# Sums of v for eight blocks a visit, and six dense matmuls in a row behind each visit

## The chip, the cores and the metric

The kernel runs on one core of a Trainium2 chip. The time is the device time of one execution in microseconds; the median of 3 runs of the kernel before is 846.09 us (845.69 to 846.45). The core has engines with a queue each that work side by side: TensorE (PE, with its weight loads shown apart as PEld), VectorE (DVE), ScalarE (ACT), GpSimd (POOL), and SyncE (SP), which issues most of the DMAs. PE writes its results to PSUM, from where DVE and ACT read them.

## The reference

Two mixers run on the same x (2048 positions, width 512) and are blended by a gate for each position. A is a Fourier transform along both axes of which the real part is kept; B is attention with 32 heads of 16 and a causal window of 256 positions. Cut to what matters:

```python
def A(x, dft_seq_re, dft_seq_im, dft_hid_re, dft_hid_im):
    a = jnp.einsum("bsd,ed->bse", x, dft_hid_re)
    b = jnp.einsum("bsd,ed->bse", x, dft_hid_im)
    return jnp.einsum("ts,bse->bte", dft_seq_re, a) - jnp.einsum("ts,bse->bte", dft_seq_im, b)

def B(x, wqkv, wo):
    # H = 32, Dh = 16, W = 256, S = 2048, D = 512
    q, k, v = split_heads(x @ wqkv)
    scores = einsum("bhqd,bhkd->bhqk", q, k) * Dh ** -0.5
    scores = where((i - j >= 0) & (i - j < W), scores, -1e9)
    o = einsum("bhqk,bhkd->bhqd", softmax(scores), v)
    return merge_heads(o) @ wo

x = A_x
g = sigmoid((x * gate_w).sum(-1, keepdims=True))
out = g * A(x, ...) + (1 - g) * B(x, B_wqkv, B_wo)
```

## The kernel before, in words

**Dense work.** Products of float32 accuracy are made of three float32r matmuls: an operand is split into `hi` (a rounded copy) and `lo` (the rest), and hi*hi, hi*lo and lo*hi are added in PSUM. The generator `dense` yields after each such matmul of 512 columns: the projections of q and k (`dqk`), of v (`dv`), of x by the hidden DFT matrices (`dab`), and then the sequence DFT (`dc`), which takes most of the kernel. The sequence matrices come in 64 pieces of 128x1024; a piece is loaded (`Pieces.load`, tile `raw`, two buffers), split into a `hi` and a `lo` tile of pool `st` (three buffers of each), and used by 24 matmuls (8 chunks of 3). The split of the next piece is put in four jobs (hi and lo of each half) that `job` hands to DVE at the matmuls 3, 9, 15 and 21 of the piece before it; in the tail the hi copies go to ACT. The first half of a piece is used by its matmuls 1 to 12, the second by 13 to 24; lo is first read by the third matmul of a half.

**Attention.** There are four groups of 8 heads and 32 blocks of 64 queries in each, 128 blocks in all, n = 0 to 127. Every block has four parts p. `s_pair(n, p)` makes scores (`s`), whose row minimum DVE finds (`sm`, line 369) and whose exponentials ACT sums (line 372): it gives the softmax's maximum and sum. 19 blocks later (`LAG`), as block k = n - 19, `t_pair(k, p)` makes the transposed scores with the maximum already in (`t`), of which ACT writes the exponentials to a tile `PT[k]` (line 450), and POOL clears what lies outside the window (lines 454, 458). `s`, `t` and a small turn of the statistics share four PSUM buffers (`ps_a`) in turn: a tile takes the buffer of the fourth before it.

**Sums of v.** `pv(k)` multiplies `PT[k]` with v in plain float32, each matmul 32 columns of the array wide (`o`, line 475), into one of two PSUM tiles of 512 queries; `v` stands for four blocks at a time in one of two tiles `vpad`, spread by POOL. `pv` is not called block by block: the main loop calls it for all blocks that have gathered, in a *visit*, at the start of block n: four blocks at first, six once the projections have ended and the tile `home` has room for some `PT`, two at the end. `PT` lies in four buffers of pool `at` and then also in two places of `home`. When eight blocks are summed, `o_out` multiplies the PSUM tile by the inverse sums (DVE, line 496) and stores it.

**Order on PE.** PE's order is the order of the program. The loop goes over n and p: `s_pair`, a gap, `t_pair`, a gap, and in each gap `fill` takes dense matmuls from the generator, two for n in 19 to 127, one or two for other n. At a visit (p = 0) both gaps come ahead of it, and `t_pair(k, 0)` stands behind it, directly ahead of the next `s_pair`. The other engines' orders are made by a scheduler, from the program's order and the helpers `behind` and `late`.

**After the attention** (`attention_done`) what is left of the sequence DFT runs with the output projection between its chunks (`tail_step`, matmuls `t` of line 922); free tiles (`vpad`, pads) take the attention's results (`oraw`).

Of the kernel before, what the change touches and what calls it, by code (L numbers as in the profile page):

```python
# [14 lines left out]
P = 128  # L15
# [17 lines left out]
def fnet_window_mix(ctx: ExitStack, tc: tile.TileContext, xT, x, wqk, wv, wr, wi, cr, ci, wo, gw, out):  # L33
    nc = tc.nc

    const = ctx.enter_context(tc.tile_pool(name="const", bufs=1))
    big = ctx.enter_context(tc.tile_pool(name="big", bufs=16))
    st = ctx.enter_context(tc.tile_pool(name="st", bufs=3))
    ev = ctx.enter_context(tc.tile_pool(name="ev", bufs=5))
# [18 lines left out]
    def f(ap):  # L58
        return ap.bitcast(F32)
# [33 lines left out]

    HALVES = slice(0, 512), slice(512, 1024)

    def load_raw(src):
# [4 lines left out]
    def split_raw(raw, act=False):  # L101
        hi = st.tile([P, 1024], F32R, name="hi")
        lo = st.tile([P, 1024], F32R, name="lo")
        for c in HALVES:
            split(hi[:, c], lo[:, c], raw[:, c], act)
        return hi, lo
# [4 lines left out]
    def split_soon(raw):  # L111
        hi = st.tile([P, 1024], F32R, name="hi")
        lo = st.tile([P, 1024], F32R, name="lo")
        for c in HALVES:
# [4 lines left out]

    def job(n):  # L120
        if n == 2 and ended:
            ended.pop(0)()
        if n % 6 == 3 and jobs:
            jobs.pop(0)()
# [22 lines left out]
    with tc.manual_schedule(engines={mybir.EngineType.Activation, mybir.EngineType.DVE, mybir.EngineType.SP}):  # L147
        wraw, *xraw = [pt_raw() for _ in range(3)]
        wq0 = [st.tile([P, 1024], F32R, name=h) for h in ("hi", "lo")]
        zero = ev.tile([P, 512], F32R, name="ev")  # L150
# [71 lines left out]
    g1 = const.tile([P, 16], F32, name="g1")  # L222
    g0 = const.tile([P, 16], F32, name="g0")
    gwb = []

# [11 lines left out]
    def gate(tb):  # L237
# [3 lines left out]
        if tb == 15:  # L241
            e = const.tile([P, 16], F32, name="ge")
# [7 lines left out]

    home = const.tile([P, 3072], F32R, name="home")
    turn = iter(range(99))
# [159 lines left out]
    PT = {}  # L412
    more = []

    VR = {}
# [108 lines left out]
    def c_part(w, chunks, ab, ps, ends):  # L524
        for i in chunks:
            if FIN and i % 2 == 0:
                tail_step()
            for n, (a, b) in enumerate(TERMS):
                nc.tensor.matmul(ps, w[a][:, i % 8 * 128:i % 8 * 128 + 128], ab[SC[i]][:, b],  # L529
                                 start=i == ends[0] and a + b == 0, stop=i == ends[1] and a == 1)  # L530
                job(i % 8 * 3 + n + 1)
                if i != chunks[-1] or a == 0:
# [50 lines left out]

    have = set()

# [9 lines left out]
    def dense():  # L595
# [83 lines left out]
        for sb in range(16):  # L679
# [280 lines left out]
    stream = dense()  # L960
    quota = 0.0

    def need(key):
# [57 lines left out]
    for n in range(N + LAG + 1):  # L1021
# [10 lines left out]
        for p in range(NP):  # L1032
            if n < N:
                s_pair(n, p)
            fill(n)
            visit = p == 0 and (k - summed >= (6 if more else 4) or k == N)
            if 0 <= k < N and not visit:
# [6 lines left out]
            if visit:  # L1044
# [68 lines left out]
```

## Time and profile before

| What | Value |
|---|---|
| median of 3 runs | 846.09 us (845.69 to 846.45) |
| the profiled execution | 845.1 us, its span 843.3 us |
| PE busy | 838.5 us, 99% |
| PEld busy | 695.8 us, 83% |
| DVE busy | 643.8 us, 76% |
| ACT busy | 611.1 us, 72% |
| POOL busy | 298.8 us, 35% |
| granted TensorE clock | 1.000 |
| DMA | 161.03 MB, mean 191 GB/s |

The span runs from the first to the last instruction. A matmul's recorded time overlaps with the next one's, since they are pipelined, so what a matmul costs is read from the distance of two starts and not from its duration. A row of the timeline has the start in us, the duration in us, the engine, the line, the operation, what it writes and reads, the shape, a count, and in brackets how long its engine sat idle before it and what ended that. Rows that follow each other with the same line and tiles are merged, with the count behind the x. Between the start of a merged row of matmuls and the next row lies what all of them took.

### The profile page before, as it was taken

Reading aid. Unit: us, or ns where it says so; the run is one execution under the profiler, and the core shown is the slowest. Engines: PE = TensorE matmul, PEld = TensorE weight load, DVE = VectorE, ACT = ScalarE, POOL = GpSimd, SP = SyncE. Lnnn points to the kernel's source line nnn. Section 1 sums busy time; section 2 is a strip of 40 time slices with the busy share of each in tenths; the row PEclk is TensorE's granted clock in tenths of the full one; section 3 lists DMA queues with packets and bytes.
Section 4 is the critical chain, followed back from the end, with each engine's and each line's share of the span. In section 5 each row is a group of like instructions: output and inputs, shape, how many; then the busy total and the mean of one; then the engine's idle time right before and its main releaser. Section 6 shows DMA issues by size and latency. Waiting matters only on the chain.

```text
span 843.3 us, 17171 instructions
## 1 busy us (share of the span) xinstructions
PE 838.5 (99%) x5310; PEld 695.8 (83%) x5310; DVE 643.8 (76%) x2083; ACT 611.1 (72%) x1832; POOL 298.8 (35%) x606
## 2 busy tenths in 40 slices
PE   9999999999999999999999999999999999999998
PEld 7888888888888888888888887878887878878997
DVE  5588978677979787787877877878987867666874
ACT  6488888878888897787877977867777865553430
POOL 8102333233232233342333243343242357756410
PEclk9999999999999999999999999999999999999999
DMA  8776678485766173534454547979874256455732
GB/s 295 251 227 187 217 243 283 159 259 202 220 222 189 54 232 107 177 120 121 140 160 126 168 153 223 298 214 309 274 216 149 96 179 198 137 192 196 220 133 92
DMA packets 94475, 161.03 MB, mean 191 GB/s; under 512 B 26800, under 2 KB 35504, under 8 KB 94384
## 3 DMA queue, kind: packets, MB, share of 16 engines
q1 hardware_dynamic: 93952, 159.28, 59.1%
q8 instruction: 42, 0.69, 0.3%
q10 hardware_dynamic: 432, 0.66, 0.2%
q14 instruction: 49, 0.40, 0.1%
HBM read 108.27 MB, written 51.64 MB: 190 GB/s over the span
## 4 chain that ended last, share of the span: by engine, by line
PE 99%; DVE 1%; issue 0%; ACT 0%; DVEq 0%; ACTq 0%
PE dc L529 42%; PE dab L304 11%; PE dqk L281 10%; PE t L449 9%; PE s L367 8%; PE o L475 8%; PE dv L304 5%; PE t L922 5%; PE s L269 1%; PE dv L593 0%; PE s L387 0%; DVE pad L350 0%; PE t L559 0%; DVE sm L369 0%; ACT sm L372 0%
## 5 line engine op out<-in xcount | busy, mean ns | idle before, releaser
L529 PE MATMUL dc<-big,hi 128*128 128x512 f32 x1020 | 344.7, 393 | 0.0
L369 DVE CUSTOM_DVE_ANT_0 sm<-s,mask 128x320 f32<-128x320 f32 (+4 forms) x512 | 235.5, 465 | 111.4 <-PE s L367 71.2
L372 ACT ACTIVATE sm<-sm,ml 128x320 f32<-128x320 f32 (+4 forms) x512 | 278.2, 544 | 56.4 <-DVE ml L369 52.1
L450 ACT ACTIVATE pt<-t 128x320 f32<-128x320 f32 (+4 forms) x392 | 159.5, 411 | 83.4 <-PE t L449 78.1
L529 PE MATMUL dc<-big,lo 128*128 128x512 f32 x510 | 200.2, 393 | 0.0
L529 PEld LDWEIGHTS dc<-big,hi 128*128 128x128 f32 x1020 | 179.3, 188 | 21.4
L454 POOL TENSOR_SCALAR_AFFINE_SELECT pt<-pt 128x128 f32<-128x128 f32 x196 | 77.1, 393 | 275.0 <-ACT pt L450 273.7
L449 PE MATMUL t<-ring,pad 128*128 128x320 f32 (+4 forms) x512 | 156.8, 306 | 0.0
L367 PE MATMUL s<-ring,pad 128*128 128x320 f32 (+4 forms) x512 | 154.9, 303 | 0.1
L350 DVE TENSOR_SCALAR pad<-ring,half 96x256 fp32r<-96x256 f32 x384 | 120.0, 359 | 5.4 <-PE t L449 4.9
L449 PEld LDWEIGHTS t<-ring,pad 128*128 128x128 f32 x512 | 96.1, 188 | 30.9 <-issue 8.7
L367 PEld LDWEIGHTS s<-ring,pad 128*128 128x128 f32 x512 | 96.2, 188 | 20.6 <-DVE ml L369 0.7
L529 PEld LDWEIGHTS dc<-big,lo 128*128 128x128 f32 x510 | 95.9, 188 | 12.0
L372 ACT ACTIVATION_READ_ACCUMULATOR sm<-sm,ml 128x1 f32 x512 | 98.1, 192 | 0.0
L588 DVE TENSOR_TENSOR lo<-raw,hi 128x512 fp32r<-128x512 f32 x137 | 94.3, 696 | 2.7 <-ACT hi L588 2.5
L304 PE MATMUL dab<-hi,big 128*128 128x512 f32 x256 | 88.9, 394 | 0.0
L281 PE MATMUL dqk<-big,hi 128*128 128x512 f32 x240 | 85.0, 393 | 0.0
L432 POOL TENSOR_SCALAR vpad<-vr,half 128x256 f32<-128x256 f32 x64 | 62.2, 983 | 62.1 <-PE o L475 29.5
L348 ACT ACTIVATE pad<-ring,half 96x256 fp32r<-96x256 f32 x128 | 66.9, 522 | 0.0
L454 POOL TENSOR_SCALAR_AFFINE_SELECT home<-home 128x128 f32<-128x128 f32 x60 | 33.8, 564 | 90.2 <-ACT home L450 85.7
L458 POOL TENSOR_SCALAR_AFFINE_SELECT pt<-pt 128x128 f32<-128x128 f32 x172 | 62.9, 366 | 0.0
L588 DVE CAST hi<-raw 128x512 fp32r<-128x512 f32 x126 | 54.3, 437 | 11.3 <-PE dc L529 10.6
(122 smaller groups left out, 1034.2 us busy)
## 6 DMA issues: line engine op xcount, KB each, us to landing
qk_scr<-home SPq DMA_DIRECT2D x32, 512.0 KB
ring<-qk_scr SPq DMA_DIRECT2D x32, 512.0 KB
raw<-cr SPq DMA_DIRECT2D x32, 512.0 KB
raw<-ci SPq DMA_DIRECT2D x32, 512.0 KB
r_scr<-ev SPq DMA_DIRECT2D x42, 256.0 KB
ab_scr<-home SPq DMA_DIRECT2D x20, 512.0 KB
big<-ab_scr SPq DMA_DIRECT2D x20, 512.0 KB
ring<-qk_scr SPq DMA_DIRECT2D x32, 256.0 KB
```

The lines of the kernel that those rows point to most:

```text
L281: nc.tensor.matmul(ps, w[a][:, c:c + 128], XT[dk, ss][:, b], start=n == 0, stop=n == 11)
L304: nc.tensor.matmul(ps, XT[dk, ss][:, a, c * 128:(c + 1) * 128], wh[b], start=n == 0, stop=n == 11)
L350: mark(f"pad{i}", nc.vector.tensor_scalar(dst, src, half[:96, h:h + 1], None, op0=OP.mult))
L367: nc.tensor.matmul(ps[:, :w], PAD[0, n][:, p], ring[1][:, p, k0:k0 + w], start=True, stop=True)
L369: mark("dve", nc.vector.tensor_tensor_reduce(out=sm[:, :w], in0=ps[:, :w], in1=mask[:, WIN - w:], scale=1.0, scalar=3e38, op0=OP.add, op1= ...
L372: mark("act", nc.scalar.activation(sm[:, :w], sm[:, :w], AF.Exp, bias=nm[:, c], scale=-1.0, accum_out=l[:, c]))
L449: nc.tensor.matmul(ps[:, :w], PAD[1, n][:, p], ring[0][:, p, q0:q0 + w], start=True, stop=True)
L450: nc.scalar.activation(pt[:, p, :w], ps[:, :w], AF.Exp, scale=-1.0)
L454: nc.gpsimd.affine_select(a, a, pattern=[[0, 2], [2, 64]], compare_op=OP.is_ge, fill=0.0, base=1, channel_multiplier=-1)
L475: nc.tensor.matmul(OT[g, sb][32 * p:32 * p + 32, q - sb * 512:e - sb * 512], v2[:, p], pt[:, p, q - q0:e - q0], start=first, stop=kb == 8 ...
L529: nc.tensor.matmul(ps, w[a][:, i % 8 * 128:i % 8 * 128 + 128], ab[SC[i]][:, b], start=i == ends[0] and a + b == 0, stop=i == ends[1] and a ...
L588: return fn(*args)
```

## The change

- A visit sums eight blocks, from a block that is a multiple of 8 on; four before that, and the last eight blocks in two visits of four. Before, it was four, then six, and two at the end.
- `PT` of the first four blocks of every eight lies in a new version of `home` (5120 columns wide instead of 3072), that of the other four in the four buffers of `at`.
- Room for it comes from pool `st`: two buffers of `hi` and of `lo` instead of three. Until the sequence DFT's first split the third pair stands in `home` (`hi_lo`); from then on there are two pairs.
- The four split jobs of a piece of the sequence DFT stand at the matmuls 6, 12, 18 and 24 of the piece before it instead of 3, 9, 15 and 21.
- `run` changes the quota of the five gaps behind a visit by +4, -1, -1, -1, -1: 6, 1, 1, 1, 1 dense matmuls instead of 2 each.
- The order in which free tiles are taken for `oraw` changes, and a small tile (`ge`) is allocated earlier.

```diff
-    st = ctx.enter_context(tc.tile_pool(name="st", bufs=3))
+    st = ctx.enter_context(tc.tile_pool(name="st", bufs=2))
...
+    splits = iter(range(999))
+
+    def hi_lo():
+        if "dc" not in have and next(splits) % 3 == 2:
+            return home[:, 3072:4096], home[:, 4096:5120]
+        return [st.tile([P, 1024], F32R, name=h) for h in ("hi", "lo")]
...
     def split_soon(raw):
-        hi = st.tile([P, 1024], F32R, name="hi")
-        lo = st.tile([P, 1024], F32R, name="lo")
+        hi, lo = hi_lo()
...
-    def job(n):
+    def job(n, at=3):
         if n == 2 and ended:
             ended.pop(0)()
-        if n % 6 == 3 and jobs:
+        if n % 6 == at and jobs:
             jobs.pop(0)()
...
-    home = const.tile([P, 3072], F32R, name="home")
+    home = const.tile([P, 5120], F32R, name="home")
...
         if p == 0:
-            if "proj" in have:
-                more.append(n)
-            c = (n - more[0]) % 6 * NP * WIN if more else 3072
-            if c + NP * WIN <= 3072:
-                PT[n] = f(home[:, c:c + NP * WIN].rearrange("p (a b) -> p a b", a=NP))
+            if "proj" in have and not more:
+                more.append(-(-n // 8) * 8)
+                pth.append(const.tile([P, 4, NP, WIN], F32, name="home", tag="home"))
+            if more and n >= more[0] and n % 8 < 4:
+                PT[n] = pth[0][:, n % 8]
             else:
                 PT[n] = at.tile([P, NP, WIN], F32, name="pt", bufs=4)
...
-                job(i % 8 * 3 + n + 1)
+                job(i % 8 * 3 + n + 1, 0)
...
             if sb == 11:
+                have.add("dc")
                 pieces.split()
...
-        for tag in ("vpad0", "vpad1", "pad1_0", "pad1_1"):
+        for tag in ("vpad0", "pad1_0", "pad1_1", "vpad1"):
...
+    run = []
...
-        quota += rate / 2
+        quota += rate / 2 + (run.pop(0) if run else 0)
...
-            visit = p == 0 and (k - summed >= (6 if more else 4) or k == N)
+            visit = p == 0 and (k - summed >= (8 if more and more[0] <= summed < N - 8 else 4))
...
                 summed = k
                 if k < N:
                     t_pair(k, p)
+                run = [4, -1, -1, -1, -1]
```

What this does to PE's order is seen at one visit in the middle of the kernel. Names: `dc` is a dense matmul of the sequence DFT, `s` and `t` the two kinds of scores, `o` the sums of v; `32x256 x4` is four matmuls of 32 columns of the array and 256 queries, each shown by the profile as two. PE before, the end of the first visit of six blocks, near 326 us, with what follows it:

```order
L475 MATMUL o<-home,vpad_301 32x64 x4
L475 MATMUL o<-home,vpad_301 32x256 x4
L475 MATMUL o<-home,vpad_300 32x320 x4
L475 MATMUL o<-pt,vpad_300 32x320 x4
L449 MATMUL t<-ring_265,pad_0_263 128x320
L367 MATMUL s<-ring_266,pad_1_262 128x320
L529 MATMUL dc<-big,lo 128x512
L529 MATMUL dc<-big,hi 128x512
L449 MATMUL t<-ring_265,pad_0_263 128x320
L529 MATMUL dc<-big,hi 128x512
L529 MATMUL dc<-big,lo 128x512
L367 MATMUL s<-ring_266,pad_1_262 128x320
```

PE now, the end of the first visit of eight blocks, with what follows it:

```order
L482 MATMUL o<-pt,vpad_301 32x256 x4
L456 MATMUL t<-ring_265,pad_0_263 128x320
L373 MATMUL s<-ring_266,pad_1_262 128x256
L536 MATMUL dc<-big,lo 128x512
L536 MATMUL dc<-big,hi 128x512 x2
L536 MATMUL dc<-big,lo 128x512
L536 MATMUL dc<-big,hi 128x512 x2
L456 MATMUL t<-ring_265,pad_0_263 128x320
L536 MATMUL dc<-big,lo 128x512
L373 MATMUL s<-ring_266,pad_1_262 128x256
L536 MATMUL dc<-big,hi 128x512
L456 MATMUL t<-ring_265,pad_0_263 128x320
```

The matmuls are the same ones and as many; a visit has grown from six blocks to eight, `t` and `s` still stand side by side behind it, and behind them six dense matmuls stand in a row, then one in each gap. Over the whole program PE now leaves the dense stream for `o` at 22 places where it did at 25.

ACT's order in the tail shows the two pairs of `hi` and `lo`. `hi<-raw` is the copy of a piece's halves, `ring<-oraw` and `ring<-pt` split the attention's results for the output projection, `pt<-t` copies its first product. ACT before, from the copies for the sixth-last piece (piece 58 of 0 to 63; its first half is DVE's) on:

```order
L588 CAST hi<-raw 128x512
L450 ACTIVATE pt<-t 128x128 x2
L450 ACTIVATE pt<-t 128x64 x4
L588 CAST hi<-raw 128x512 x2
L80 CAST ring_265<-oraw 128x256
L80 CAST ring_266<-pt 128x3x256
L80 CAST ring_265<-pt 128x256
L931 COPY pt<-t 128x256
L588 CAST hi<-raw 128x512 x2
```

ACT now, from the copies for the same piece 58 on:

```order
L594 CAST hi<-raw 128x512 x2
L81 CAST ring_266<-pt 128x3x256
L81 CAST ring_265<-pt 128x256
L938 COPY pt<-t 128x256
L594 CAST hi<-raw 128x512 x2
```

Where the copies for piece 60 stood, behind the first `COPY`, those for piece 59 stand now: the splits of the tail have moved back by one piece against the work around them.

More of the change, by code (lines that the diff above doesn't have):

```diff
@@ L36, in fnet_window_mix @@
     const = ctx.enter_context(tc.tile_pool(name="const", bufs=1))
+    have = set()
     big = ctx.enter_context(tc.tile_pool(name="big", bufs=16))
-    st = ctx.enter_context(tc.tile_pool(name="st", bufs=3))
+    st = ctx.enter_context(tc.tile_pool(name="st", bufs=2))
     ev = ctx.enter_context(tc.tile_pool(name="ev", bufs=5))
@@ L111, in split_soon @@
     def split_soon(raw):
-        hi = st.tile([P, 1024], F32R, name="hi")
-        lo = st.tile([P, 1024], F32R, name="lo")
+        hi, lo = hi_lo()
         for c in HALVES:
@@ L148, in fnet_window_mix @@
         wraw, *xraw = [pt_raw() for _ in range(3)]
-        wq0 = [st.tile([P, 1024], F32R, name=h) for h in ("hi", "lo")]
+        wq0 = hi_lo()
         zero = ev.tile([P, 512], F32R, name="ev")
@@ L223, in fnet_window_mix @@
     g0 = const.tile([P, 16], F32, name="g0")
+    ge = const.tile([P, 16], F32, name="ge")
     gwb = []
@@ L241, in gate @@
         if tb == 15:
-            e = const.tile([P, 16], F32, name="ge")
+            e = ge
             nc.scalar.activation(e, gl, AF.Exp, scale=-1.0)
@@ L413, in fnet_window_mix @@
     more = []
+    pth = []
     VR = {}
@@ L581, in c_half @@
         yield
-    have = set()
     def late(fn, *args):
```

## The prediction

> **What bounds the kernel now.** I read the page first (busy shares, the slices with the clock, the chain that ended last), then PE's waits, then the chain in order of time.
>
> ```profile
> span 843.3 us, 17171 instructions
> PE 838.5 (99%) x5310; PEld 695.8 (83%) x5310; DVE 643.8 (76%) x2083; ACT 611.1 (72%) x1832; POOL 298.8 (35%) x606
> PEclk9999999999999999999999999999999999999999
> PE 99%; DVE 1%; issue 0%; ACT 0%; DVEq 0%; ACTq 0%
> ```
>
> ```profile
> PE dv L593 <- DVE ev L151: 1.5, 1, 1.5
> ```
>
> The chain is PE for 99% of the span, at full clock, and the list of PE's waits has one row, at the start. So the time is the sum of the distances between matmul starts, and a change is worth what it takes out of that sum, minus any wait that it makes. The number of matmuls stays, as the order shows; what changes is how many visits there are and what stands beside what. The chain in order of time shows the visits:
>
> ```profile
> 118.23 2.29 PE o L475 x32
> ...
> 291.60 2.29 PE o L475 x32
> 323.08 3.39 PE o L475 x80
> ...
> 726.79 3.39 PE o L475 x80
> ```
>
> Visits of four blocks run until 292 us, of six from 323 us on. By the code that is nine of four (36 blocks), fifteen of six (90) and one of two: 25. The change makes ten of four (40 blocks; 40 is the first multiple of 8 after the projections end), ten of eight (to 120) and two of four: 22, as the order has it.
>
> **The change: fewer visits.** What a visit costs beside its own matmuls is read at one of them, in PE's timeline:
>
> ```profile
> 322.01 0.39 PE L529 MATMUL dc<-big,hi 128*128 128x512 f32 x1
> 322.24 0.39 PE L529 MATMUL dc<-big,lo 128*128 128x512 f32 x1
> 322.46 0.61 PE L529 MATMUL dc<-big,hi 128*128 128x512 f32 x2
> 323.01 1.84 PE L475 MATMUL o<-pt,vpad 128*32 128x256 f32 x48
> 324.66 1.26 PE L475 MATMUL o<-home,vpad 128*32 128x64 f32 x24
> 325.74 0.72 PE L475 MATMUL o<-pt,vpad 128*32 128x320 f32 x8
> 326.39 0.41 PE L449 MATMUL t<-ring,pad 128*128 128x320 f32 x1
> 326.65 0.30 PE L367 MATMUL s<-ring,pad 128*128 128x320 f32 x1
> 326.79 0.39 PE L529 MATMUL dc<-big,lo 128*128 128x512 f32 x1
> 327.02 0.39 PE L529 MATMUL dc<-big,hi 128*128 128x512 f32 x1
> 327.24 0.31 PE L449 MATMUL t<-ring,pad 128*128 128x320 f32 x1
> 327.39 0.39 PE L529 MATMUL dc<-big,hi 128*128 128x512 f32 x1
> ...
> 327.84 0.31 PE L367 MATMUL s<-ring,pad 128*128 128x320 f32 x1
> ```
>
> Start to start, a dense matmul takes 0.22 to 0.23 us (322.01, 322.24, 322.46, so the fourth starts at 322.69) and a `t` or `s` of 320 columns 0.15 (327.24 to 327.39). Three distances are longer at the visit. Into it: 322.69 to 323.01 is 0.32, 0.09 more than a dense matmul. Out of it: the last block's matmuls take 0.65 (325.74 to 326.39), where a block inside a visit takes 0.55 (two blocks more make 3.39 out of 2.29): 0.10. And `t` directly ahead of `s`: 0.26 (326.39 to 326.65) instead of 0.15: 0.11. Together 0.30 us a visit. The blocks themselves are only moved. Three visits fewer: 3 x 0.30 = 0.9 us less, all on PE's chain. I take it at full value, since the three transitions look the same at visits of four and six blocks; a gain of nothing or of twice that is no row's reading.
>
> **Six dense in a row, then one in each of four gaps.** The dense matmuls are as many, so only the neighbours change. In a row they take 0.225 each (322.01 to 322.69). A lone dense matmul between `t` and `s` is in no row; its nearest are the pair 0.15 + 0.22 = 0.37 above, and the weight loads:
>
> ```profile
> L449 PEld LDWEIGHTS t<-ring,pad 128*128 128x128 f32 x512 | 96.1, 188 | 30.9 <-issue 8.7
> ...
> 343.40 0.19 PE L367 MATMUL s<-ring,pad 128*128 128x64 f32 x1
> 343.43 0.47 PE L529 MATMUL dc<-big,hi 128*128 128x512 f32 x1
> ```
>
> Two loads of 0.188, strictly one behind the other, make 0.376 for a pair. That is one end: 0.006 x 88 pairs = 0.5 us. The other is a gain of 0.01 a pair (0.8 us in all): two columns of digits cannot tell it. Behind a 64-column `s` (343.40) PE goes on after 0.03, so loads run ahead of matmuls: I take 0.
>
> **Who must keep up.** The row of six holds back the tiles behind a visit by four dense matmuls (0.9 us), and the lone ones bring them in again, 0.37 apart instead of 0.60. `t` and `s` share four buffers, so a tile needs its fourth predecessor to be read. ACT at the same visit:
>
> ```profile
> 326.91 0.44 ACT L450 ACTIVATE pt<-t 128x320 f32<-128x320 f32 x1 [3.32 <-PE t L449]
> 327.63 0.57 ACT L372 ACTIVATE sm<-sm,ml 128x320 f32<-128x320 f32 x1 [0.29 <-DVE ml L369]
> ...
> 328.19 0.42 ACT L450 ACTIVATE pt<-t 128x320 f32<-128x320 f32 x1
> 337.80 0.67 ACT L696 ACTIVATE ev<-dc,g 128x512 f32<-128x512 f32 x1
> ```
>
> ACT has nothing to do in a visit (3.32 us idle) and starts from an empty queue. By these rows: dense from 326.79, six of 0.226, so the second `t` at 328.15, then `s` 328.52, `t` 328.90, `s` 329.27, `t` 329.65, and from there 0.60 apart as before: `s` 330.25, `t` 330.85. An `s` reaches ACT 0.98 after its start (326.65 to 327.63), and the exponentials of the next `t` follow 0.56 later and take 0.42. The `t` of 328.90 is therefore read by 329.50 + 0.56 + 0.42 = 330.48, and its buffer is wanted at 330.85: 0.37 us to spare, the least of the row (the `t` of 328.15 is read by 329.1 and wanted at 329.65). A store of the sequence DFT (0.67 us, one per 48 dense matmuls, about every 14 us) that falls between eats that and costs 0.3; ten visits have such stores beside them, and the wait of the exponential is some 2 us long, one seventh of 14: 10 / 7 x 0.3 = 0.4 us at most, 0 at least. I take 0.1, nearer to 0, since a store counts only where it stands directly ahead of that one exponential. What is queued behind ACT's late exponential is the next `sm`, then PE's tiles.
>
> **Two pairs of hi and lo.** A split job now stands three dense matmuls later and needs the matmuls of the piece two before to be over. In the attention a dense matmul takes 0.30 us of the loop (0.60 from 327.24 to 327.84 has two). The last lo half goes out at matmul 24 and is read 15 later: 4.5 us; it was 5.4. A lo half on DVE, then the last copies on ACT and the matmul that first needs them:
>
> ```profile
> 338.21 0.69 DVE L588 TENSOR_TENSOR lo<-raw,hi 128x512 fp32r<-128x512 f32 x1
> ...
> 792.71 1.15 ACT L588 CAST hi<-raw 128x512 fp32r<-128x512 f32 x2 [0.18 <-PE dc L529]
> 806.13 1.14 ACT L588 CAST hi<-raw 128x512 fp32r<-128x512 f32 x2 [2.95 <-PE dc L529]
> 832.25 0.40 PE L529 MATMUL dc<-big,hi 128*128 128x512 f32 x1
> ```
>
> 0.69 of 4.5 leaves 3.8 us of cover for DVE's queue: it costs nothing. The next load of `raw`, behind the split on SP, moves by the same 0.9 us as the split that needs it. In the tail the splits run as far ahead as the buffers let them: the last copies at 806.13, their piece's matmuls from 832.25. With a pair less every split waits for one piece more (806.13 - 792.71 = 13.4 us), as the order shows, and 832.25 - 806.13 - 13.4 = 12.7 us remain: nothing again. If DVE's backlog ever passed 3.8 us, PE would stop at a piece's third matmul.
>
> The rest (other tiles for `oraw`, `ge` allocated earlier, `PT` in `home`) adds no instruction. `PT` of the last block of a visit has seven blocks' matmuls ahead of it instead of five, and both `vpad` tiles are refilled within three blocks of a visit, of eight.
>
> **Sum.** -0.9 + 0 + 0.1 + 0 = -0.8 us. The profiled execution (845.1, 1.8 of it outside the span) would become 844.3; it lies 1.0 under the median, so the median comes to 845.3 us. I call 0.2%, 1.7 us, the least that a measurement of this kernel tells from no change.
>
> **Rivals.**
>
> 1. Slower: the tiles behind a visit wait. The place is the third `t` behind a visit, with its 0.37 us to spare. Against it: the empty queue at 326.91. For it: in the stage of the first visits ACT has less room than above.
>
> ```profile
> 118.10:140.10 22.00, 22.00 (x131) 17.67 (x130) 18.28 (x64) 19.69 (x61) 7.33 (x20) 1.00 0.67 231
> 323.00:355.30 32.30, 32.30 (x227) 26.80 (x226) 24.00 (x90) 24.82 (x82) 9.91 (x27) 1.00 0.39 128
> ```
>
> ACT (the fourth) is busy 19.69 of 22.00 us there, 24.82 of 32.30 later. If each of the 22 visits loses one split's time, 0.69 - 0.37 = 0.3, it costs 6.6 us: 846.1 - 0.9 + 6.6 = 851.8; if the ten early ones alone, 848.2. It ends slower from 0.04 us a visit on, and by over 0.2% from 0.12.
>
> 2. Faster by more: PE's own small waits go as well. The starts have gaps too small for the list of waits, such as these two, first and last of five places from 136 to 568 us, 0.9 us together:
>
> ```profile
> 136.04 0.74 PE L304 MATMUL dab<-hi,big 128*128 128x512 f32 x2
> 136.63 0.31 PE L367 MATMUL s<-ring,pad 128*128 128x320 f32 x1
> ...
> 567.55 0.40 PE L529 MATMUL dc<-big,hi 128*128 128x512 f32 x1
> 567.88 0.38 PE L449 MATMUL t<-ring,pad 128*128 128x320 f32 x1
> ```
>
> (567.55 to 567.88 is 0.33 instead of 0.23.) If the new order frees all of them: 846.1 - 1.8 = 844.3. The lone pairs at their lower end give as much.
>
> 3. A split comes late, in the attention, where the cover was worked out as 3.8 us: a wait of 0.5 us in ten pieces would make 5 us, 850.2.
>
> 4. The clock falls in the longer visits. A visit of eight lasts 3.39 + 2 x 0.55 = 4.5 us. Behind one of 3.39 us the dense matmuls are at once 0.22 apart (326.79, 327.02) and the clock's digits never fall. At the start of the kernel eight matmuls took 3.70 us, 0.46 each instead of 0.225:
>
> ```profile
> 1.51 3.70 PE L593 MATMUL dv<-ev 128*128 128x512 f32 x8 [1.51 <-DVE ev L151]
> ```
>
> If each of the ten visits of eight left PE in that state for as long, it would cost 10 x 1.9 = 19 us: 864. [...]
>
> **Chances.** The forecast, 844.4 to 847.0: 0.58. Rival 1: 0.17, most of it slower by over 0.2%. Rival 2: 0.17. Rival 3: 0.06. Rival 4: 0.02. So faster by over 0.2%: 0.17; within: 0.60; slower: 0.23. The range takes in rival 2 and the early part of rival 1: 843.7 to 848.2.
>
> **What would show it.** Right: 22 stretches of `o` in the chain; the same three distances at each; two starts 0.37 apart behind them; a span near 842.5; no new row among PE's waits. Wrong: a `t` or `s` behind a visit with a start over 0.1 us late, released by ACT or DVE (rival 1); a dense matmul at the head of a piece released by DVE line 594 (rival 3); a clock under 1.00 or dense starts 0.45 apart behind visits of 4.5 us (rival 4); gaps like that at 567.55 gone (rival 2).

## The result, and the profile after

The changed kernel takes 847.53 us (median of 17 runs, 846.20 to 848.47); the kernel before, on the same chip, took 846.00 (17 runs). The ratio is 1.0020, with a 95% interval of 1.0013 to 1.0027: 1.1 to 2.3 us slower. The forecast was 0.8 us faster. The outer range of 843.7 to 848.2 holds the time, but its upper part stood for waits behind the early visits, which are not what came.

The profiled execution took 847.0 us, its span 844.9. From the page of the changed kernel:

```profile
PE 839.8 (99%) x5310; PEld 697.6 (83%) x5310; DVE 644.0 (76%) x2082; ACT 609.0 (72%) x1833; POOL 296.9 (35%) x606
...
PEclk9999999999999999999999999999999999999999
...
PE 98%; DVE 1%; issue 0%; ACT 0%; DVEq 0%; ACTq 0%
```

PE's waits in the same profile:

```profile
PE dv L599 <- DVE ev L156: 1.5, 1, 1.5
PE t L929 <- DVE rt L933: 0.3, 1, 0.3
```

The granted clock is 1.000 as before, PE is still the chain, and one short wait is new. (Lines are 6 or 7 further down than before: the score matmuls `t` are L456, `s` L373, the sums of v L482, the sequence DFT L536, the matmuls of the tail L929.) The visits are the 22 that were forecast; their stretches in the chain begin and end with these:

```profile
118.80 2.29 PE o L482 x32
...
355.33 4.46 PE o L482 x96
398.55 4.46 PE o L482 x96
...
744.29 2.60 PE o L482 x32
759.98 1.22 PE o L482 x32
```

One of them with the row behind it, in the timeline of PE and ACT:

```profile
398.16 0.39 PE L536 MATMUL dc<-big,hi 128*128 128x512 f32 x1
398.48 2.36 PE L482 MATMUL o<-home,vpad 128*32 128x320 f32 x32
...
402.94 0.41 PE L456 MATMUL t<-ring,pad 128*128 128x320 f32 x1
403.19 0.31 PE L373 MATMUL s<-ring,pad 128*128 128x320 f32 x1
403.34 0.39 PE L536 MATMUL dc<-big,hi 128*128 128x512 f32 x1
...
404.72 0.31 PE L456 MATMUL t<-ring,pad 128*128 128x320 f32 x1
404.75 0.67 ACT L703 ACTIVATE ev<-dc,g 128x512 f32<-128x512 f32 x1
404.87 0.39 PE L536 MATMUL dc<-big,hi 128*128 128x512 f32 x1
405.10 0.31 PE L373 MATMUL s<-ring,pad 128*128 128x320 f32 x1
...
405.48 0.31 PE L456 MATMUL t<-ring,pad 128*128 128x320 f32 x1
```

Into the visit 0.32 (398.16 to 398.48), `t` to `s` 0.25, and eight blocks in 4.46 instead of the 4.49 forecast: the three distances are the same, and the three visits fewer are worth 0.9 us. The visit of four blocks at 744 us gives a third of it back: it takes 2.60 where the one at 118 us takes 2.29. The weight loads of its last block stand still twice, for 0.15 and 0.17 us, the second time until POOL has cleared that block's `PT` (PEld is PE's weight loads):

```profile
746.15 0.14 PEld L482 LDWEIGHTS o<-home,vpad 128*32 128x32 f32 x4 [0.17 <-POOL home L465]
```

The second profile of the changed kernel (a run below) has the same two gaps. Over all visits PE takes 0.6 us less than before, not 0.9. In the row, the six dense matmuls take 1.38 (403.34 to 404.72), a lone pair 0.38.

**Where the time came from.** For every start on PE the distance to the next was set against the commonest distance of its kind (same matmul, same neighbours), the visits left out, and the excess summed by the stage of the program. Two profiles of each kernel (the second ones are runs below), in us:

```
stage                                  before          changed
to 97 us, ahead of the first visit     4.36   4.80     5.01   5.04
t of blocks 0 to 35                    2.70   2.65     2.96   2.95
t of blocks 36 to 71                   1.91   1.83     2.87   2.88
t of blocks 72 to 95                   2.21   2.19     1.92   2.02
t of blocks 96 to 119                  0.75   0.75     0.90   0.81
t of blocks 120 to 127                 0.84   0.84     0.90   2.06
the tail                               0.38   0.38     0.97   0.87
```

The first stage says nothing: ahead of 97 us the order of work is the same but for the place of the third pair, and over all profiles below it came out anywhere from 4.36 to 5.41. Three rows stand out: blocks 36 to 71 with 1.0 us, the tail with 0.5, and blocks 120 to 127 with 0.1 to 1.2. (The wait inside the visit at 744 us is in no row, since the visits are left out.)

*Blocks 36 to 71* have no wait. The groups by shape between 457 and 482 us, where neither kernel has a visit, show it; first the kernel before, then the changed one (mean recorded ns behind the busy time):

```profile
L529 PE MATMUL dc<-big,hi 128*128 128x512 f32 x56 | 19.5, 390 | 0.0
```

```profile
L536 PE MATMUL dc<-big,hi 128*128 128x512 f32 x54 | 19.0, 395 | 0.0
```

Each dense matmul is recorded 5 ns longer, and in the same 25 us fewer get done. The starts say the same: before, a tile and two dense matmuls take 0.146 + 0.228 + 0.226 = 0.600 us, here 0.611 to 0.614. There are two cadences, and a stretch keeps to one of them. In the changed kernel the slow one goes from 427 to 492 us, in the kernel before from 426 to 442.

*The tail.* The new wait at 782.88 hangs on a chain over four engines. The timeline of the changed kernel, with what released each in brackets:

```profile
771.93 0.74 POOL L883 TENSOR_TENSOR pt<-oraw 128x256 f32<-128x256 f32 x1 [7.86 <-DMA oraw<-o_scr]
...
778.41 1.05 ACT L81 CAST ring<-pt 128x1024 fp32r<-128x1024 f32 x1 [4.62 <-POOL pt L886]
...
779.50 1.35 DVE L86 TENSOR_TENSOR ring<-pt,ring 128x1024 fp32r<-128x1024 f32 x1 [3.11 <-ACT ring L81]
...
782.88 0.98 PE L929 MATMUL t<-ring 128*128 128x256 f32 x6 [0.27 <-DVE rt L933]
```

In the kernel before the same steps stand at 769.77, 776.71 and 777.80, and no `t` waits:

```profile
769.77 0.74 POOL L876 TENSOR_TENSOR pt<-oraw 128x256 f32<-128x256 f32 x1 [3.50 <-PE dc L529]
...
777.80 1.36 DVE L85 TENSOR_TENSOR ring<-pt,ring 128x1024 fp32r<-128x1024 f32 x1 [2.41 <-ACT ring L80]
```

POOL's first sum is 2.2 us later, though PE reaches the tail only 1.0 later, and it waits for a load, not for PE. SP's issues, the kernel before and then the changed one:

```profile
752.85 0.91 SPq L56 DMA_DIRECT2D rt<-r_scr  x2
757.16 0.33 SPq L56 DMA_DIRECT2D raw<-ci  x1
...
761.31 0.38 SPq L56 DMA_DIRECT2D o_scr<-ev  x1
...
764.50 2.15 SPq L56 DMA_DIRECT2D oraw<-o_scr  x4
```

```profile
756.60 0.91 SPq L57 DMA_DIRECT2D rt<-r_scr  x2
757.60 0.41 SPq L57 DMA_DIRECT2D raw<-ci  x1
758.06 0.90 SPq L57 DMA_DIRECT2D rt<-r_scr  x2
...
762.59 0.51 SPq L57 DMA_DIRECT2D o_scr<-ev  x1
...
767.06 0.92 SPq L57 DMA_DIRECT2D oraw<-o_scr  x2
```

The last loads of `oraw` read what the store `o_scr<-ev` writes; they go out 4.5 us behind it instead of 3.2, and the store itself goes out 1.3 later. The loads of `rt` have moved closer to that store: the first two, at 752.85 before, go out at 756.60, still ahead of `raw`, and two more stand directly behind `raw`, at 758.06, where the kernel before issued them one by one at 760.72 and 761.75.

### The profile page after: what moved, and what is told of

The parts are those of the page before. It is cut to its first block, busy times and chain, and to the rows that moved or that the text cites. A ratio compares the mean times of both kernels' runs of the same rounds, so it can differ in the third digit from the quotient of the medians.

```text
span 844.9 us, 17176 instructions
## 1 busy us (share of the span) xinstructions
PE 839.8 (99%) x5310; PEld 697.6 (83%) x5310; DVE 644.0 (76%) x2082; ACT 609.0 (72%) x1833; POOL 296.9 (35%) x606
## 4 chain that ended last, share of the span: by engine, by line
PE 98%; DVE 1%; issue 0%; ACT 0%; DVEq 0%; ACTq 0%
PE dc L536 42%; PE dab L310 10%; PE dqk L287 10%; PE t L456 9%; PE s L373 8%; PE o L482 8%; PE dv L310 5%; PE t L929 5%; PE s L275 1%; PE dv L599 0%; PE s L393 0%; DVE pad L356 0%; PE t L566 0%; DVE sm L375 0%; ACT sm L378 0%
## 5 line engine op out<-in xcount | busy, mean ns | idle before, releaser
L536 PE MATMUL dc<-big,hi 128*128 128x512 f32 x1020 | 345.4, 394 | 0.0
L536 PE MATMUL dc<-big,lo 128*128 128x512 f32 x510 | 200.5, 393 | 0.0
L536 PEld LDWEIGHTS dc<-big,hi 128*128 128x128 f32 x1020 | 179.8, 188 | 22.4
L457 ACT ACTIVATE pt<-t 128x320 f32<-128x320 f32 (+4 forms) x336 | 133.9, 402 | 39.7 <-PE t L456 38.0
L461 POOL TENSOR_SCALAR_AFFINE_SELECT pt<-pt 128x128 f32<-128x128 f32 x168 | 65.2, 388 | 264.2 <-ACT pt L457 262.5
L456 PE MATMUL t<-ring,pad 128*128 128x320 f32 (+4 forms) x512 | 156.5, 306 | 0.0
L373 PE MATMUL s<-ring,pad 128*128 128x320 f32 (+4 forms) x512 | 155.1, 303 | 0.1
L456 PEld LDWEIGHTS t<-ring,pad 128*128 128x128 f32 x512 | 96.1, 188 | 27.6 <-issue 7.6
L457 ACT ACTIVATE home<-t 128x320 f32<-128x320 f32 x176 | 74.6, 426 | 56.8 <-PE t L456 55.1
L373 PEld LDWEIGHTS s<-ring,pad 128*128 128x128 f32 x512 | 96.2, 188 | 19.4 <-DVE ml L375 0.7
L536 PEld LDWEIGHTS dc<-big,lo 128*128 128x128 f32 x510 | 95.9, 188 | 13.2
L594 DVE TENSOR_TENSOR lo<-raw,hi 128x512 fp32r<-128x512 f32 x134 | 92.6, 699 | 2.1 <-ACT hi L594 2.0
L461 POOL TENSOR_SCALAR_AFFINE_SELECT home<-home 128x128 f32<-128x128 f32 x88 | 42.4, 482 | 84.1 <-ACT home L457 82.0
L310 PE MATMUL dab<-home,big 128*128 128x512 f32 x192 | 62.3, 393 | 0.0
L594 DVE CAST hi<-raw 128x512 fp32r<-128x512 f32 x122 | 51.9, 432 | 8.3 <-PE dc L536 8.3
```

What stands on the lines that cost most here:

```text
L310: nc.tensor.matmul(ps, XT[dk, ss][:, a, c * 128:(c + 1) * 128], wh[b], start=n == 0, stop=n == 11)
L373: nc.tensor.matmul(ps[:, :w], PAD[0, n][:, p], ring[1][:, p, k0:k0 + w], start=True, stop=True)
L456: nc.tensor.matmul(ps[:, :w], PAD[1, n][:, p], ring[0][:, p, q0:q0 + w], start=True, stop=True)
L457: nc.scalar.activation(pt[:, p, :w], ps[:, :w], AF.Exp, scale=-1.0)
L461: nc.gpsimd.affine_select(a, a, pattern=[[0, 2], [2, 64]], compare_op=OP.is_ge, fill=0.0, base=1, channel_multiplier=-1)
L594: return fn(*args)
```

## The experiments

**The changed kernel once more.** No edit.

> The changed kernel once more, for its profile. In the first profile of it the three visits saved their 0.9 us, and some 2.5 us came in elsewhere: about 0.65 before any visit (up to 97 us), about 0.6 behind the attention (a tile t at 782 us waits 0.4 for DVE), about 0.3 in the lone pairs, and 1.2 in stretches where every dense matmul takes 0.006 us more for tens of us. If these belong to the program, all four recur at the same places within 0.2 us. If the stretches are a matter of one execution, their sum (5.0 us, against 3.8 before) comes out elsewhere between 3.5 and 5.5 and their places differ. Time 847.5 in both cases.

847.39 us (11 runs; ratio 1.0020, 1.0011 to 1.0028). The slow stretch of 427 to 492 us is there again within 0.1 us, and those from 341, 514 and 599 us within 0.6, while others moved (35 to 75 in one, 35 to 95 in the other): most of them belong to the program. New is a wait at the end of the attention, on ACT and PE:

```profile
753.10 0.62 ACT L81 CAST ring<-oraw 128x512 fp32r<-128x512 f32 x1 [3.08 <-DMA oraw<-o_scr]
...
754.00 0.33 PE L456 MATMUL t<-ring,pad 128*128 128x128 f32 x1 [0.92 <-ACT pt L457]
```

A copy for the output projection stands on ACT ahead of the exponentials and its load has not landed; PE's next `t` comes 1.1 us late. In the first profile the load was 1.4 us earlier, and no `t` waited. In the kernel before, the same copy stands at 755.26, ahead of exponentials of 128 columns; it waits 1.26 us for its load there, and no `t` waits.

**Without the row.**

```diff
-                run = [4, -1, -1, -1, -1]
+                run = []
```

> The changed kernel without the row: two dense matmuls in each gap behind a visit, as before. Theory A (the row and its lone dense matmuls cost the time): the 0.3 us of the lone pairs and what waits they make are gone, 846.6 or less. Theory B (the two pairs of hi and lo with their later jobs cost it): 847.5, as with the row. Theory C (the cost is at the two ends of the kernel, where tiles and loads are ordered otherwise): 847.2 to 847.5, and the waits before 97 us and at 782 us stay.

847.52 (ratio 1.0022, 1.0012 to 1.0033). Theory A falls for the changed kernel: it is as slow without the row. (Its profile has a wait of 0.7 us on ACT's copy at 753 us, of the kind above, so what the row alone costs is not read from it.) The slow stretch from 427 us is there too, up to 477.7, where it ends at a wait of 0.15 us ahead of an `s`.

**The row in the kernel before.**

```diff
-        quota += rate / 2
+        quota += rate / 2 + (run.pop(0) if run else 0)
...
                 if k < N:
                     t_pair(k, p)
+                run = [4, -1, -1, -1, -1]
```

> The kernel before with the row alone: visits of four and six as before, 25 of them, behind each six dense matmuls and then one in each of four gaps. Theory A: slower than the kernel before by 0.4 to 1.0 us, 846.4 to 847.0 (100 lone pairs at 0.003 each are 0.3, and any waits behind them). Theories B and C: 846.0 to 846.3.

847.46 (ratio 1.0023, 1.0014 to 1.0032): there the row costs more than theory A said. Its profile has places like this one, 5 us behind a visit (PE and ACT):

```profile
655.65 0.63 PE L529 MATMUL dc<-big,hi 128*128 128x512 f32 x2
...
655.82 0.41 ACT L450 ACTIVATE pt<-t 128x320 f32<-128x320 f32 x1
656.29 0.41 PE L449 MATMUL t<-ring,pad 128*128 128x320 f32 x1
```

Two dense matmuls take 0.64 instead of 0.46, because the `t` behind them waits until that exponential has ended (656.23). With its neighbour 0.29 us are lost here, 0.43 at 524 us, where DVE's row minimum and ACT's exponential end the waits, 0.22 at 397, where the profile names no releaser, and 0.33 at 305, where a turn of the statistics waits for DVE: 1.3 us. (The profiled execution, 846.71, is the fastest of its eleven and lies 1.1 to 1.6 us above those of the kernel before.) At 524 and 655 us that is the forecast's first rival, in the kernel that it was not meant for.

**Two pairs of hi and lo alone.**

```diff
-    st = ctx.enter_context(tc.tile_pool(name="st", bufs=3))
+    st = ctx.enter_context(tc.tile_pool(name="st", bufs=2))
...
-        hi = st.tile([P, 1024], F32R, name="hi")
-        lo = st.tile([P, 1024], F32R, name="lo")
+        hi, lo = hi_lo()
...
-                job(i % 8 * 3 + n + 1)
+                job(i % 8 * 3 + n + 1, 0)
```

> The kernel before with two pairs of hi and lo instead of three, the third in a tile of its own until the sequence DFT begins, and the split jobs at the matmuls 6, 12, 18 and 24; the visits, the places of PT of six blocks and the gaps as before. Theory B: slower by all that the change lost, 2.0 to 2.5 us, 848.0 to 848.5. Theory A: 846.0. Theory C: 846.0 to 846.6, the part of it that comes before 97 us, since the third pair lies elsewhere there.

(The third pair stands in columns 3072 to 5119 of a wider `home`, as in the changed kernel, and not in a tile of its own.) 846.51 (ratio 1.0007, 0.9998 to 1.0015, which holds no change). Theory B falls as the whole cause. From block 36 to the end of the attention the excess is that of the kernel before (5.6 us against 5.6 and 5.7); the tail has 0.80 instead of 0.38, with a wait at 782 us. So that part of the loss belongs to the pairs, as far as one profile shows.

**One break.** In block n = 84, behind the visit at 441 us, one gap is emptied and the next takes four.

```diff
+            if (n, p) == (84, 0):
+                run = [0, -2, 2]
```

> The changed kernel with one gap emptied and the next doubled: behind the visit at 441 us, in the second block after it, one tile t stands directly ahead of the next s, and four dense matmuls follow. In both profiles of the changed kernel the dense matmuls take 0.006 us more each from 427 to 492 us, 1.1 us in all, of it 1.0 behind that visit. Theory D (a cadence that short tiles start and that stays until the next irregularity in the stream): the break ends it near 446 us, dense matmuls take 0.226 from there on, and the time falls by 1.0 less the 0.1 of the break, 846.5. Theory E (those matmuls are slower there for another reason, such as the transfers beside them): the stretch goes on to 492 us, 847.5 to 847.6.

846.72 (ratio 1.0012, 1.0003 to 1.0020), 0.8 less than the changed kernel. PE at the break:

```profile
449.07 0.31 PE L456 MATMUL t<-ring,pad 128*128 128x320 f32 x1
449.22 0.31 PE L373 MATMUL s<-ring,pad 128*128 128x320 f32 x1
449.37 0.40 PE L536 MATMUL dc<-big,lo 128*128 128x512 f32 x1
```

and the group between 457 and 482 us:

```profile
L536 PE MATMUL dc<-big,hi 128*128 128x512 f32 x56 | 19.3, 390 | 0.0
```

The slow stretch ends at 450.7 instead of 492.6, and blocks 36 to 71 lose 2.18 instead of 2.87: theory D. The break costs nothing: `t` to `s` is 0.15 there (449.07 to 449.22), so the 0.25 at a visit (403.19 less 402.94) comes with the `o` ahead of the `t`, not with `t` and `s` as neighbours.

**Visits elsewhere.**

```diff
-                more.append(-(-n // 8) * 8)
+                more.append(-(-n // 8) * 8 + 4)
...
-            visit = p == 0 and (k - summed >= (8 if more and more[0] <= summed < N - 8 else 4))
+            visit = p == 0 and (k - summed >= (8 if more and more[0] <= summed < N - 12 else 4))
```

> The changed kernel with its visits of eight from a block on that is 4 more than a multiple of 8, and three visits of four at the end: 23 visits instead of 22, and none directly behind a group's last, short tiles. Theory D: the slow stretch that begins at 427 us ends at 443, as in the kernel before, 1.0 less, and a visit more costs 0.3: 846.8. Theory E: the stretch to 490 us stays, 847.8. What happens at the very end (a wait at 752 us in one profile of two, one at 782) may move by up to 0.5 either way, since the visits there are others.

The stretch did what theory D says: 428 to 442.7, and the one that begins at 598 ended at 616 instead of 648. The time did not: 848.89 (5 runs, 847.26 to 849.91; ratio 1.0041, 1.0027 to 1.0054). The profile of 847.26 shows a wait of its own (DVE and PE):

```profile
540.72 0.43 DVE L594 CAST hi<-raw 128x512 fp32r<-128x512 f32 x1 [1.72 <-DMA raw<-cr]
...
541.61 0.41 PE L373 MATMUL s<-ring,pad 128*128 128x320 f32 x1 [0.53 <-DVE ml L375]
```

A split stands on DVE before its load has landed, and an `s` on PE waits until DVE has read an earlier one; and the excess of the tail is 1.6, against 0.4 in the kernel before. The profiled execution is the fastest of the five, 1.6 us under their median, so that what makes the others slow is not shown.

**The last eight blocks as six and two.**

```diff
-            visit = p == 0 and (k - summed >= (8 if more and more[0] <= summed < N - 8 else 4))
+            visit = p == 0 and (k - summed >= (8 if more and more[0] <= summed < N - 8 else 6 if summed == N - 8 else 4) or k == N)
```

> The changed kernel with its last eight blocks in a visit of six and one of two, as in the kernel before, instead of four and four. Theory F (the last visit, of four instead of two blocks, ends later by 1.1 us, and with it the store, the loads and the sums that the first tiles t of the tail hang on; and the visit at 744 us lets ACT reach a copy of oraw before its load has landed): the wait at 782 us (0.4 to 0.5) and that at 752 us (0, 0.7 and 1.1 in three profiles) are both gone, 846.5. Theory G (it is the two pairs of hi and lo that make the tail late; with them alone the wait at 782 was 0.3): the wait at 782 stays at 0.3 or more, 847.0 to 847.4.

847.90 (ratio 1.0027, 1.0017 to 1.0036). PE's waits:

```profile
PE o L482 <- POOL pt L461: 0.7, 1, 0.7
PE t L929 <- DVE rt L933: 0.3, 1, 0.3
```

There is no wait at 752 us, as in the first profile of the changed kernel; ACT's copy stands at 755.41 again, close to its place in the kernel before. The last visit waits 0.7 for POOL to clear the last block's `PT`. The wait at 782 stays: it does not hang on the last visit, as theory G has it, though the time lies above that theory's 847.4 too.

**The kernel before once more.** No edit.

> The kernel before once more, for its profile. If the slow stretches of dense matmuls belong to the program, they recur at 426 to 442, 600 to 652 and the other places of the first profile, their sum 3.8 us within 0.4, and nothing is slow from 443 to 480. If they are a matter of chance, places differ by tens of us. The phase before the first visit (0 to 97 us) differs by up to 1 us between executions, as it did between four profiles of kernels with the same order there (4.4 to 5.4 us over the common base).

845.62 (one run). The stretches 426 to 442 and 600 to 652 us recur, and from 443 to 480 nothing is slow; the sum is 4.0 (3.8 in the first). One other stretch begins at 494 instead of 481, so a part is chance.

**A break in the kernel before.** There the visit at 614 us stands directly behind a group's short tiles.

```diff
+            if p == 0 and n == 116:
+                run = [0, -2, 2]
```

(with the quota's line of the row).

> The kernel before with one gap emptied and the next doubled, in block n = 116, right behind the visit at 614 us: one t stands directly ahead of the next s. In both profiles of the kernel before the dense matmuls behind that visit, which stands directly behind a group's last short tiles, take 0.235 and 0.232 us in turn with 0.147 of a tile (0.614 in all, instead of 0.600) until the visit at 646 us. Theory D (the slow cadence stays until the next irregularity): the break ends it near 622 us; 24 us of it less are 0.55, less 0.1 for the break, 0.45 us faster than the kernel before, 845.15. Theory E (something else beside them makes them slow): the stretch goes on to 652 us, and the break costs 0.1: 845.7.

The groups between 623 and 644 us, the kernel before and then this one:

```profile
L529 PE MATMUL dc<-big,hi 128*128 128x512 f32 x47 | 16.5, 396 | 0.0
```

```profile
L529 PE MATMUL dc<-big,hi 128*128 128x512 f32 x47 | 16.2, 390 | 0.0
```

The stretch ends at 622.5 instead of 652: theory D. 845.11 us, 0.3 less than the kernel before beside it (845.45); the ratio, 0.9992 (0.9983 to 1.0001), makes it 0.7. The excess of blocks 96 to 119 falls by 0.5. All are near the 0.45 of the theory, but the interval holds no change.

**Two breaks in the changed kernel.**

```diff
+            if p == 0 and n in (84, 116):
+                run = [0, -2, 2]
```

> The changed kernel with two such breaks, in the blocks n = 84 and n = 116, behind the visits at 441 and 614 us, the two visits that stand directly behind a group's last short tiles. Theory D: the slow stretches 451 to 492 and 619 to 648 are gone, 0.7 and 0.5 us less with the breaks' own cost: 846.2 to 846.4. Theory E: 847.6.

846.31 (ratio 1.0011, 1.0002 to 1.0020). The stretches end at 451 and 622.5, as theory D said, and the number is in its range; but the kernel before took 845.45 beside it, and the ratio is hardly under the 1.0012 of one break. The 0.5 us of the second break are read in the stretch, not shown in the time.

**The third pair back in the tail.** On the run of the pairs alone (`third` is a tile of its own, of 2048 columns, and `FIN` is set when the attention has ended):

```diff
-        if "dc" not in have and next(splits) % 3 == 2:
-            return home[:, 3072:4096], home[:, 4096:5120]
+        if ("dc" not in have or FIN) and next(splits) % 3 == 2:
+            return third[:, :1024], third[:, 1024:]
```

> The kernel before with two pairs of hi and lo in the attention, as in the run of the pairs alone (0.6 us slower than the kernel before, of which 0.4 lay in the tail, with the wait at 782 us), but with the third pair again in use from the end of the attention on. Theory G (the tail's wait comes from the missing third pair): the wait at 782 us is gone, the tail is 0.4 us shorter, 846.0. Theory H (it comes from the loads of the output projection, which are issued and land later, and not from the splits): the wait stays at 0.3, 846.4.

846.66 (ratio 1.0014, 1.0005 to 1.0023), and the tail loses 1.44, with waits at 776 and 782 us. Theory G falls, H stands: giving the pair back does not help. On SP `raw` stands ahead of the two loads of `rt` here too.

**The order of two loads.** On the run of the pairs alone, the first two loads of `rt` are no longer held back on SP:

```diff
-            with behind("sp"):
+            with behind(*(("sp",) if i else ())):
```

> The run with the pairs alone, with the first two loads of rt free to go when the scheduler wants, so that on SP they stand ahead of the load of raw at 757 us again, as in the kernel before. Theory I (two pairs change SP's order there; the two loads of rt then run beside the attention's last store, which lands 0.9 us later, and the loads of oraw behind it, POOL's sums and ACT's copies follow): the last loads of oraw go out 3.3 us behind the store as before, not 4.1, the wait at 782 us (0.23 and 0.10) is gone, 0.4 us faster than with the pairs alone, 846.0. Theory J (it is the later split jobs or a chance of DMA): the wait stays, 846.4.

SP with the pairs alone, and then now:

```profile
757.22 0.34 SPq L57 DMA_DIRECT2D raw<-ci  x1
757.67 1.87 SPq L57 DMA_DIRECT2D rt<-r_scr  x2
```

```profile
753.57 0.92 SPq L57 DMA_DIRECT2D rt<-r_scr  x2
...
757.63 0.33 SPq L57 DMA_DIRECT2D raw<-ci  x1
...
762.03 0.38 SPq L57 DMA_DIRECT2D o_scr<-ev  x1
...
765.60 2.37 SPq L57 DMA_DIRECT2D oraw<-o_scr  x4
```

845.70 us, ratio 0.9999 (0.9991 to 1.0008), 0.8 less than with the pairs alone, though the two intervals overlap; the tail's excess is 0.383 instead of 0.80, that of the kernel before, and no `t` waits. The last loads of `oraw` go out 3.6 us behind the store instead of 4.1, not quite the 3.3 expected. Theory I: what two pairs cost in the tail comes from SP's order.

**Both mended in the changed kernel.** The two breaks, and the same line for the loads of `rt`.

> The changed kernel with the two breaks (846.3) and with the same two loads of rt ahead of the load of raw. Theory I: the wait at 782 us (0.43 and 0.10) is shorter or gone, 845.8. Theory J: 846.3. In this kernel the last visit has four blocks and ends 1 us later than the kernel before's, which these loads do not change, so that a rest of the wait may stay.

845.46 us, ratio 0.9996 (0.9987 to 1.0005), 2.0 less than the changed kernel by the two ratios, whose intervals do not touch. The loads of `rt` now go out at 746.27 and at 755.86, all four ahead of the load of `raw` at 756.90. The tail has 0.384, the store is 3.1 us ahead of the last loads of `oraw`, and in its profile blocks 120 to 127 have 0.91 with no wait.

**And without the row.** The same with `run = []`.

> The changed kernel with the two loads of rt ahead of the load of raw, the two breaks, and without the row of six: visits of eight, two dense matmuls in every gap behind them. If the row's lone dense matmuls cost what the rows of the traces show (73 of them at 0.004 more each, and their neighbours), it is 0.3 to 0.6 us faster than with the row, 844.9 to 845.2, and faster than the kernel before by as much. If the row costs nothing, 845.5.

845.48, ratio 1.0005 (0.9996 to 1.0014). The medians with and without the row are the same, and by the ratios the kernel without it is 0.8 us slower, within the two intervals; its profile has a wait on ACT's copy at 753 us, 0.6 us, which the one with the row has not. No cost and no gain of the row is shown. None of these kernels is shown to be faster than the kernel before.

## Why the prediction was wrong

- *Three visits fewer, -0.9.* Right in the main: 22 visits, and the three distances of 0.32, 0.65 less 0.55, and 0.25 are there. The third is not the price of `t` beside `s`, as the step has it: at the breaks these stand 0.15 apart, and 0.25 behind the `o` of a visit. And 0.3 of the 0.9 is lost again in the visit at 744 us.
- *"The blocks themselves are only moved."* This step failed, and it decides the sign. Visits of eight from a multiple of 8 on put one visit (441 us) directly behind a group's last short tiles, besides the one at 614 us that stood there already. In all eleven profiles with a visit at 614 us and no break behind it, the slow cadence that the short tiles bring outlived that visit, to 647 us or later; at 441 us it did so in all four profiles with a visit there and no break (to 478 or 492 us), while in the eight without a visit there it was over by 443. Cost: 1.0 us, of which one break took 0.7 away. The forecast's 0.22 to 0.23 for a dense matmul hid the two cadences in its rounding.
- *Two pairs, "nothing again" in the tail.* Wrong by 0.4 to 0.6. The splits were not late, as forecast. But the pairs changed SP's order: two loads of `rt` went behind `raw` with the pairs alone, and in the changed kernel four of them stand around `raw` just ahead of the attention's last store. The last loads of `oraw` then went out later behind that store. The step asked whether the splits had cover and not which other loads on SP change places; one line that lets the first loads of `rt` go earlier ends the wait in both kernels. In the attention the pairs cost nothing, as forecast.
- *The end as two visits of four* was not costed. Its first visit, at 744 us, waits 0.3 in both profiles, for POOL at least in part. And ACT's copy of `oraw` comes 2 to 3.5 us earlier than before, ahead of the exponentials of 192 columns: 0 and 1.1 us in the two profiles of the changed kernel, 0.7 without the row. With six and two the copy is back near its old place, but a visit waits 0.7 for POOL.
- *The row and the lone pairs, 0.* The lone pair came at the upper end of its bounds, 0.377 in the mean. Yet the kernels without the row are no faster, so nothing speaks against 0 for the sum; it is not shown either, since their profiles have another wait in its place.
- *ACT behind the visits, 0.1, and rival 1.* At 404.75 the store of the sequence DFT fell directly on the row, and the tiles after it still stood 0.38 apart. In the kernel before, the same row did make such waits: with a turn's and one of unknown cause they lost 1.3 us.
- *Rival 2.* Of the small gaps, the one at 567.55 is gone in both profiles, and blocks 72 to 95 have 0.2 less; others came.
- *Rival 3.* No split of the changed kernel came late for its own matmul.
- *Rival 4.* Visits of 4.46 us left the clock at 1.000 and dense matmuls 0.23 apart (403.34, 403.57). (The rival's price was too high in any case: the eight matmuls at the start take 3.54 us to the next start, at 5.05, and not the recorded 3.70.)

The sum by the profiles: -0.9 for the visits, +0.3 for the wait in the one at 744 us, +1.0 for blocks 36 to 71, +0.5 for the tail, about +0.5 for the copy on ACT, +0.3 in blocks 0 to 35, of which no run tells the cause, and -0.2 in blocks 72 to 95: +1.5, as measured. That it comes out so closely is luck in part, since the copy's 0.5 is a middle of 0 and 1.1, and the first stage, 0.2 to 0.7 higher in the changed kernel, is left out. With cadence and tail mended the changed kernel is at -0.3 us (-1.1 to +0.4), where the forecast had -0.8; but one of its two breaks is worth about 0.5 by the profile in the kernel before as well, so that a gain of the visits by themselves was read in the distances and not shown in a time.

## What to carry to other kernels

Where PE is the chain for 99% of the time, "only moved" can have a price of its own, here 1.0 us in blocks 36 to 71: read what the moved block will stand beside, above all short matmuls, and compare the mean of the same matmul in several windows, to the nanosecond. When a change frees or takes buffers, follow each DMA queue's new order for every load that shares it, not only the ones whose buffers change (SP's order cost 0.4 us of the tail with the pairs alone). Losses of half a microsecond show in two profiles of each kernel, stage by stage, when the medians alone cannot place them.

## What was not expected of the hardware

A stream of matmuls of 512 columns with 320-column tiles between them runs in one of two cadences at the same granted clock of 1.000: 0.600 us for a tile and two dense matmuls, or 0.611 to 0.614, and in the slow one each dense matmul is recorded as 395 or 396 ns instead of 390. Where it was followed, the slow one came with tiles of fewer than 320 columns and ended with them if the ordinary stream followed directly (426 to 442 us in the kernel before); with a visit directly behind them it lasted 30 to 50 us more, until some irregularity (in the changed kernel the row behind the visit at 484 us and a turn of the statistics at 648, without the row a wait of 0.15 us at 477), or until a break of four dense matmuls behind a `t` and an `s`, which ended it at all eight places where one was set. Not every irregularity ends it: in the changed kernel it outlived a turn at 475 us. Nor does it need such short tiles: it ran from 480 to 489 us in the kernel before, from 494 to 510 in its second profile and from 568 to 587 with the pairs alone, and what started it there is not known. What keeps it going is not shown by any run here. Start to start, a dense matmul takes 226 to 228 ns in the one (the kernel before, 457 to 480 us) and 231 to 236 in the other (the changed kernel, 450 to 474 us).
